# Squared-ReLU attention with routed rows: a table of engines and places for single slots of the middle batches

## The chip, the cores and the metric

One core of a Trainium2 chip runs the whole program. The metric is the device time of one execution in microseconds (us); smaller is better. The engines named below are PE (TensorE matmul, with PEld for its weight loads), ACT (ScalarE), DVE (VectorE), POOL (GpSimd) and SP (SyncE, which issues nearly all transfers).

## The reference, cut to what matters

The inputs are u and v (8 x 3136 x 256), z (8 x 3136 x 64) and the weights of a small network.

```python
scores = (1.0 / S) * np.matmul(z, z.transpose(0, 2, 1))
attn = np.maximum(scores, 0.0) ** 2
x = u * np.matmul(attn, v)
...
for b in range(B):
    top_idx = np.argpartition(-(x[b] @ w_gate), capacity)[:capacity]     # capacity = 128
    xe = x[b, top_idx]
    ye = np.maximum(xe @ w1, 0.0) @ w2
    out[b, top_idx] = xe + sigmoid(xe @ w_gate)[:, None] * ye
```

Nearly all of the arithmetic is in attn times v. The scores matrix is symmetric, so each off-diagonal block of attn is needed twice, once as it is and once transposed.

## The kernel before, in words

**Chunks and slots.** The work goes batch by batch (8 batches). A batch has 7 chunks of output columns: 0 to 4 are 512 wide, 5 is 256 and 6 is 320 wide. A chunk has 13 slots, so a batch has 91, and a slot's number within its batch is its place. Twelve slots of a chunk take two 128-row tiles of v each, the thirteenth takes the last 64 rows. "First batch" is batch 0, "fourth batch" is batch 3.

**One slot.** Products are made in about full precision from a high part and a low part. For a new slot, `scores(k)` has PE make the scores (tile `sc`, one buffer in PSUM), ACT applies ReLU into `a` (line 515) and writes its square, rounded, as the high part `hi` (L525). The exact square is then made in place in `a`, on ACT (L531) or on DVE (L535). `low(k)` makes the low part `lo = a - hi` on POOL or on DVE (both L615) and, where the block is needed again, transposes it on DVE (L578) for a store to `squares`. In the diagonal slot of a chunk (`is_first`) the block is its own mirror, with transposes of its own (L596). For an old slot `old_scores(k)` has the squares fetched back by a transfer into `qk`; ACT makes `hi` from it (L474) and there is no square to make. PE then multiplies into `acc` (L642): 16 matmuls with `hi` and 8 with `lo` in a two-tile slot.

**Order.** The order on every engine is the order in which the program calls the operations; each engine runs its own queue in that order. The main loop goes over the slots. In slot k it runs the plan's loads and preparations, then `mix(k, ...)`, which issues slot k's matmuls and, between them, `scores(k + 3)`. After that come the stores, and the "posts" of the slot with the low parts of slot k + 3 in their middle:

```python
        half = (len(posts) + 1) // 2
        now = settle_scores
        posts = [*posts[:half], now, *posts[half:]]
```

`settle_scores` first makes the squares that were left to DVE, then for each slot its transposes and its low part. In the last two slots of a chunk posts are held over to the next slot.

**Which engine.** A ledger `busy` holds planned microseconds of backlog for ACT, DVE and POOL; `spend` adds to it and each slot takes its own length off. The exact square goes to ACT where ACT's backlog is below DVE's plus 1.0 plus the square's own price. A low part goes to DVE where POOL's backlog would come out 1.2 above DVE's.

**Closing work of a chunk.** In its last two slots `finish_early` scales half of the sums on ACT (L723, two instructions), and `finish` adds the rest on DVE and multiplies by u (L736 and L737, two pairs), which frees the accumulators. What remains goes on the list `near` as two tasks: two transposes to rows on DVE (L746) with a multiply on POOL (L755) and the stores; and a sum on DVE (L764) for the gate. They are taken at slots 2 and 5 of the next chunk (`k % SLOTS % 3 == 2`).

**Routing.** When a batch is finished, `route` and `expert` put its routing and its small network on the list `far`: rounds of a count (DVE, L952 and L958) and a settling, then matmuls. Tasks of `far` are taken in later slots that have no task of `near`, usually every other slot. The first count reads `gates`, which a pair of transfers brings (out at L935, back at L944).

**Preparations.** `prep_v(b, g)` splits a tile of v into its parts, the copy on ACT (L125, 0.6 us) and the rest on POOL (L126); `bring_z(b, c)` does the same for a chunk's moving operand. Both stand in the plan at fixed slots.

Of the kernel before, what the change touches and what calls it, by code (L numbers as in the profile page):

```python
# [22 lines left out]
LEAD = 3  # L23
# [4 lines left out]
BITS = 4  # L28
INT_MIN = -(1 << 31)


# [57 lines left out]
def attention_then_routed_ffn(ctx: ExitStack, tc: tile.TileContext, zt, ut, v, wg, w1, w2, cst, cst16, keys, outs, at, cap):  # L89
# [259 lines left out]
    def prep_v(b, g, on=None, hi_on=None):  # L349

        st = staged["v", b, g // 2][:, g % 2 * 2 :]
        n = 2 if 2 * g < NJ else 1
        if n == 2:
            t = vpool.tile([P, 2, NK, 2 * P], F32R, name="V", tag="V")
        else:
            t = vpool.tile([P, 2, NK, P], F32R, name="Vr", tag="Vr", bufs=1)
        src = st[:, :n].rearrange("p a d -> p (a d)").rearrange("p (f h i) -> p h f i", h=NK, i=Q)
        parts_of = [t[:, w].rearrange("p h (f i) -> p h f i", i=Q) for w in range(2)]
        hi_on = hi_on or on
        lo_on, took = on or nc.gpsimd, {"dve": 1.0} if on else {"pool": 2.3} if hi_on else {"act": 0.6, "pool": 1.3}  # L360
        if not on and b == 0 and n == 2 and busy["pool"] + 1.3 > busy["dve"] + 0.6:
            lo_on, took = nc.vector, {"act": 0.6, "dve": 0.6}
        split(src, *parts_of, hi_on and hi_on.tensor_copy, lo_on.tensor_tensor)
        for q in range(n):
            V[b, 2 * g + q] = t[:, :, :, q * P : (q + 1) * P]
        spend(**took)
# [47 lines left out]
    def is_second(k):  # L414

        b, c, js, _ = slots[k]
        return (b or c) and c < WHOLE and js[0] == c * GT + 2

    parts = {}
    lows = []  # L420
    held_turns = []
    near = deque()
# [55 lines left out]
    def scores(k):  # L478
# [50 lines left out]
        dve = 0.15 + 0.00208 * w  # L529
        if busy["act"] < busy["dve"] + 1.0 + dve + (0.16 + 0.00236 * w if turns(k) else 0.0):  # L530
            nc.scalar.activation(a, a, AF.Square)  # L531
            spend(act=act)
            square = lambda: None
        else:
            square = lambda: nc.vector.tensor_tensor(a, a, a, op=ALU.mult)  # L535
            spend(dve=dve)
# [6 lines left out]
    def low(k, a, hi, pieces, square):  # L543
# [55 lines left out]

        later = 2 * (0.08 + 0.00118 * w) if k >= LEAD and k % (SLOTS * NCH) == 1 else 0.0  # L600
        if k < LEAD or later:
            held_turns.append(lambda: (spend(dve=-later), turned()))
        else:
            turned()
        spend(dve=later)
        if n == 2:
            lo = work.tile([P, 2, CH], F32R, name="lo", tag="lo", bufs=LEAD)[:, :, within(c, k % SLOTS in ((0, 1, 8) if b == B - 1 else (0, 1)))]
            for view, src in pieces:
# [3 lines left out]
                dve = 0.05 + 0.001 * of  # L612
                if busy["pool"] + took > busy["dve"] + dve + (1.2 if busy["pool"] > 0 else 0.0):
                    on, took = nc.vector, dve
                on.tensor_tensor(view(lo), src, view(hi).bitcast(F32), op=ALU.subtract)  # L615
                spend(**{"dve" if on is nc.vector else "pool": took})
        parts[k] = (hi, lo)

# [826 lines left out]
    for b in range(B):  # L1445
        k0 = b * per

        for i in range(NCH):
# [4 lines left out]
            else:  # L1453
                k = k0 - 1 + 4 * (i - WHOLE)
            use = lambda b=b, i=i: prep_z(b, i)
# [8 lines left out]
        for g in range(NJ // 2 + 1):  # L1464
            k = k0 - 10 + 3 * g // 2 if b else max(1, g - 3)
            if b or g > 3:
# [7 lines left out]
        for c in range(NCH):  # L1474
            if b or c:
                at_slot(k0 + c * SLOTS - LEAD - 4, lambda b=b, c=c: bring_z(b, c))
                if c < WHOLE:
# [121 lines left out]
    for k, (b, c, js, is_old) in enumerate(slots):  # L1599
# [8 lines left out]
        if len(js) == 2:  # L1608
            if near and (k % SLOTS or c <= NCH - late if late else k % SLOTS % 3 == 2):
                tasks.append(near.popleft())  # L1610
# [28 lines left out]
        if late and k == len(slots) - 1:  # L1639
            held.reverse()  # L1640
            (f0, s0), (f1, s1) = held
            for op in f0[0][0][:3]:
                op()
        mix(k, [op for ops, _ in tasks for op in ops], lambda: more_scores(k + LEAD))
        settle_turns()
# [94 lines left out]
```

## Time and profile before

| what | us |
|---|---|
| three runs, median (lowest to highest) | 2106.46 (2103.55 to 2107.81) |
| the profiled execution | 2098.54 |
| its span, first to last instruction | 2096.7 |
| PE busy in it | 2024.4 |
| DVE, ACT, POOL busy in it | 1504.4, 1487.4, 1302.3 |

The profile shows one execution, by the chip's clock. An instruction's idle time is how long its engine stood still just before it, and the arrow names what ended the wait. PE's matmuls of one group overlap, so a group's time is that of the group. The middle batches repeat each other nearly to the hundredth of a microsecond, so one batch can stand for the six.

### The profile page before, as it was taken

The page shows a single profiled execution, that of the slowest core. Times are in us where ns is not written, and L with a number is a line of the kernel's source. Part 1 is how long each engine was busy: PE and PEld are TensorE (multiplying, and loading weights), DVE is VectorE, ACT ScalarE, POOL GpSimd, SP SyncE. Part 2 cuts the span into 40 slices and gives each one's busy share as a digit, 9 for nine tenths or more (in the row PEclk, how much of TensorE's full clock was granted, in tenths as well). Part 3 has the DMA queues.
Part 4 walks back from the last instruction along what each step waited for, and adds up shares of the span by engine and source line. Part 5 has one row for each costly group of instructions (what it writes and reads, how often), then busy time and mean ns, then how long its engine had stood idle before and what let it go on. Part 6 is the DMA issues. An engine that isn't in the chain of part 4 may idle for free.

```text
span 2096.7 us, 51099 instructions
## 1 busy us (share of the span) xinstructions
PE 2024.4 (97%) x19700; PEld 1682.5 (80%) x19700; DVE 1504.4 (72%) x2646; ACT 1487.4 (71%) x2028; POOL 1302.3 (62%) x716
## 2 busy tenths in 40 slices
PE   8999999999999999999999999999999999999998
PEld 5788977779787797777977788777887878777787
DVE  9777678756786568865788657885678865866675
ACT  7776688666886578765788657876578766877553
POOL 5765478735786367763678536784467754775643
PEclk9999999999999999999999999999999999999999
DMA  6788767786678966788668886678766777666852
GB/s 178 214 232 223 226 183 226 231 240 192 184 210 225 239 184 185 220 226 224 171 195 222 233 220 190 192 219 229 213 200 198 205 193 212 197 171 178 216 155 93
DMA packets 450868, 426.94 MB, mean 204 GB/s; under 512 B 136576, under 2 KB 377792, under 8 KB 447808
## 3 DMA queue, kind: packets, MB, share of 16 engines
q1 hardware_dynamic: 449488, 421.18, 71.3%
q8 instruction: 154, 2.52, 0.5%
q0 software_dynamic: 768, 2.10, 0.3%
q14 instruction: 90, 0.74, 0.1%
q10 hardware_dynamic: 368, 0.39, 0.1%
HBM read 248.94 MB, written 174.60 MB: 202 GB/s over the span
## 4 chain that ended last, share of the span: by engine, by line
PE 54%; DMA 9%; issue 7%; POOL 7%; ACT 6%; DVE 6%; SPq 5%; POOLq 0%; ACTq 0%; DVEq 0%
PE acc L642 46%; POOL lo L615 5%; PE sc L511 5%; DMA zst<-in_zt 2%; DVE a L535 2%; ACT a L515 2%; ACT hi L525 2%; DMA squares_narrow<-aT 1%; DVE aT L578 1%; SPq L753 1%; DMA qk<-squares 1%; DMA ut<-in_ut 1%; PE y L1402 1%; SPq L446 1%; ACT a L531 1%
## 5 line engine op out<-in xcount | busy, mean ns | idle before, releaser
L642 PE MATMUL acc<-hi,V 64*128 64x512 f32 (+2 forms) x10752 | 1242.5, 362 | 6.8 <-DVE ut L737 4.8
L642 PEld LDWEIGHTS acc<-hi,V 64*128 64x128 f32 x10752 | 952.1, 185 | 171.2 <-issue 13.0
L615 POOL TENSOR_TENSOR lo<-a,hi 128x1024 fp32r<-128x1024 f32 (+1 forms) x280 | 640.2, 2289 | 417.5 <-DVE a L535 173.2
L642 PE MATMUL acc<-lo,V 64*128 64x512 f32 (+2 forms) x5376 | 694.9, 362 | 34.0 <-POOL lo L615 33.6
L642 PEld LDWEIGHTS acc<-lo,V 64*128 64x128 f32 x5376 | 486.1, 185 | 121.2 <-POOL lo L615 52.8
L515 ACT ACTIVATE a<-sc 128x1024 f32<-128x1024 f32 (+2 forms) x345 | 326.8, 947 | 225.8 <-PE sc L511 193.3
L578 DVE STREAM_TRANSPOSE aT<-a 128x512 f32<-128x512 f32 (+1 forms) x494 | 316.2, 680 | 167.7 <-ACT a L531 162.6
L474 ACT CAST hi<-qk 128x1024 fp32r<-128x1024 f32 (+2 forms) x327 | 279.1, 856 | 156.4 <-PE acc L642 112.5
L615 DVE TENSOR_TENSOR lo<-qk,hi 128x1024 fp32r<-128x1024 f32 (+2 forms) x216 | 318.0, 1483 | 68.9 <-ACT hi L474 54.4
L525 ACT ACTIVATE hi<-a 128x1024 fp32r<-128x1024 f32 (+2 forms) x345 | 339.8, 985 | 27.7 <-PE acc L642 5.4
L615 POOL TENSOR_TENSOR lo<-qk,hi 128x1024 fp32r<-128x1024 f32 (+2 forms) x111 | 222.0, 2007 | 128.5 <-ACT hi L474 92.0
L531 ACT ACTIVATE a<-a 128x1024 f32<-128x1024 f32 (+2 forms) x268 | 263.4, 983 | 7.6
L535 DVE TENSOR_TENSOR a<-a 128x1024 f32<-128x1024 f32 (+1 forms) x77 | 135.2, 1756 | 43.6 <-ACT hi L525 38.1
L755 POOL TENSOR_TENSOR ut<-x,w_run 128x1024 f32<-128x1024 f32 (+2 forms) x52 | 130.3, 2506 | 54.6 <-DVE x L746 52.6
L126 POOL TENSOR_TENSOR V<-vst,V 128x512 fp32r<-128x512 f32 x92 | 147.4, 1612 | 23.7 <-ACT V L125 23.7
L736 DVE SCALAR_TENSOR_TENSOR acc<-acc,x 128x512 f32<-128x512 f32 (+2 forms) x112 | 70.0, 625 | 78.7 <-PE acc L642 78.7
L126 POOL TENSOR_TENSOR ZL<-zst,ZH 64x256 fp32r<-64x256 f32 x70 | 69.2, 988 | 70.4 <-ACT ZH L125 52.7
L511 PE MATMUL sc<-Z,ZH 64*128 64x512 f32 x480 | 97.5, 394 | 12.7 <-ACT a L515 12.0
L511 PE MATMUL sc<-Z,ZL 64*128 64x512 f32 x480 | 92.8, 372 | 0.8 <-DVE ZL L126 0.8
L511 PE MATMUL sc<-Zl,ZH 64*128 64x512 f32 x480 | 92.5, 373 | 0.0
L615 DVE TENSOR_TENSOR lo<-a,hi 128x1024 fp32r<-128x1024 f32 (+2 forms) x65 | 75.7, 1165 | 16.7 <-ACT a L531 16.6
L723 ACT ACTIVATE x<-acc 128x512 f32<-128x512 f32 (+2 forms) x112 | 54.4, 538 | 45.3 <-PE acc L642 42.0
(220 smaller groups left out, 1753.0 us busy)
## 6 DMA issues: line engine op xcount, KB each, us to landing
squares<-aT SPq DMA_DIRECT2D x160, 512.0 KB, 3.4
qk<-squares SPq DMA_DIRECT2D x320, 256.0 KB, 6.4
squares_narrow<-aT SPq DMA_DIRECT2D x320, 128.0 KB, 4.3
qk<-squares_narrow SPq DMA_DIRECT2D x80, 512.0 KB, 4.3
out<-x SPq DMA_DIRECT2D x162, 128.0 KB, 3.4
ut<-in_ut SPq DMA_DIRECT2D x40, 512.0 KB, 5.9
vst<-in_v SPq DMA_DIRECT2D x158, 128.0 KB, 3.1
zmv<-in_zt SPq DMA_DIRECT2D x78, 128.0 KB, 4.3
```

The lines of the kernel that those rows point to most:

```text
L126: (lo_on or nc.vector.tensor_tensor)(lo, src, hi.bitcast(F32), op=ALU.subtract)
L474: nc.scalar.copy(by(hi), src)
L511: nc.tensor.matmul(ps[:, q, :w], stationary(high, js[0] // 2, q), mov[m][rows], start=i == 0, stop=i == 2)
L515: nc.scalar.activation(a, ps[:, :, :w], AF.Relu)
L525: nc.scalar.activation(pieces[0][0](hi), pieces[0][1], AF.Square)
L531: nc.scalar.activation(a, a, AF.Square)
L535: square = lambda: nc.vector.tensor_tensor(a, a, a, op=ALU.mult)
L578: nc.vector.transpose(to, a[:, q].rearrange("p (m t a) -> p m t a", m=GT, a=Q))
L615: on.tensor_tensor(view(lo), src, view(hi).bitcast(F32), op=ALU.subtract)
L642: nc.tensor.matmul(bank[g][h][:, cols[g]], V[b, j][rows, i, h], mov[rows], start=(b, c, g, h) not in opened, stop=len(js) == 1 and n == 2,)
L736: nc.vector.scalar_tensor_tensor(rest, rest, SCALE * SCALE, sums[h], op0=ALU.mult, op1=ALU.add)
L755: nc.gpsimd.tensor_tensor(wx, runs, consts["wg_run"].rearrange("p (o r) -> p o r", o=1).broadcast_to([P, NB, RUN]), op=ALU.mult,)
```

## The change

For batches 1 to 6 (the middle ones) a table `PICK` overrides what the ledger or the rule would say in single places: `lo` (True: the low part on DVE, False: on POOL) in eleven, `sq` (True: the exact square on ACT, False: on DVE) in five, `ne` (take a task of `near` or not) in seven, `tl` (True: the transposes are issued behind the low part) in six. Its keys are places, 0 to 90. The ledger still books what is done, so later choices can differ too.

A flag `within_end` is set in the main loop when slot k is one of the last two of its chunk. The scores made there are those of places 1 and 2 of the next chunk; where these are new slots, the exact square goes to ACT, in all batches, unless `PICK` says otherwise.

Two preparations of v move (`VP`: number 8 two slots earlier, number 12 one slot earlier) and `bring_z` of chunk 4 moves two slots later (`BZ`), in all batches but the first. `VD` and `ZP` are all zeros.

```diff
+PICK = {
+    "lo": {
+        1: {1: True, 3: False, 8: True, 11: True, 23: True, 33: True, 44: True, 57: False, 66: False, 69: True, 76: True},
+    },
+    "ne": {
+        1: {4: True, 13: True, 41: False, 42: True, 65: False, 79: True, 83: False},
+    },
+    "sq": {
+        1: {1: False, 3: False, 6: False, 17: True, 48: False},
+    },
+    "tl": {
+        1: {6: True, 8: True, 26: True, 31: True, 46: True, 56: True},
+    },
+}
+VP = [0, 0, 0, 0, 0, 0, 0, 0, -2, 0, 0, 0, -1]
...
+BZ = [0, 0, 0, 0, 2, 0, 0, 0]
...
+    def pick(kind, k, default):
+        b, at = divmod(k, SLOTS * NCH)
+        return PICK.get(kind, {}).get(0 if b == 0 else 2 if b == B - 1 else 1, {}).get(at, default)
...
-        if busy["act"] < busy["dve"] + 1.0 + dve + (0.16 + 0.00236 * w if turns(k) else 0.0):
+        on_act = within_end[0] or busy["act"] < busy["dve"] + 1.0 + dve + (0.16 + 0.00236 * w if turns(k) else 0.0)
+        if pick("sq", k, on_act):
...
+        behind = (turns(k) or is_first(k)) and pick("tl", k, False)
         if k < LEAD or later:
             held_turns.append(lambda: (spend(dve=-later), turned()))
-        else:
+        elif not behind:
             turned()
...
-                if busy["pool"] + took > busy["dve"] + dve + (1.2 if busy["pool"] > 0 else 0.0):
+                if pick("lo", k, busy["pool"] + took > busy["dve"] + dve + (1.2 if busy["pool"] > 0 else 0.0)):
...
+        if behind and not (k < LEAD or later):
+            turned()
...
-            k = k0 - 10 + 3 * g // 2 if b else max(1, g - 3)
+            k = k0 - 10 + 3 * g // 2 + (VP[g] if 0 < b else 0) if b else max(1, g - 3)
...
-                at_slot(k0 + c * SLOTS - LEAD - 4, lambda b=b, c=c: bring_z(b, c))
+                at_slot(k0 + c * SLOTS - LEAD - 4 + (BZ[c] if b else 0), lambda b=b, c=c: bring_z(b, c))
...
-            if near and (k % SLOTS or c <= NCH - late if late else k % SLOTS % 3 == 2):
+            if near and (k % SLOTS or c <= NCH - late if late else pick("ne", k, k % SLOTS % 3 == 2)):
...
+        within_end[0] = k % SLOTS >= SLOTS - 2
         mix(k, [op for ops, _ in tasks for op in ops], lambda: more_scores(k + LEAD))
```

## Rows read from the trace of the kernel before

**Rows 1.** The page, part 1: busy time of each engine.

```profile
PE 2024.4 (97%) x19700; PEld 1682.5 (80%) x19700; DVE 1504.4 (72%) x2646; ACT 1487.4 (71%) x2028; POOL 1302.3 (62%) x716
```

**Rows 2.** Busy time by stretch, the whole fourth batch; length, then each engine.

```profile
781.20:1038.90 257.70, 250.47 (x2455) 208.36 (x2453) 183.17 (x325) 184.81 (x252) 161.71 (x88) 1.00 0.74 209
```

**Rows 3.** Waits of PE over the span: total, times, longest.

```profile
PE acc L642 <- POOL lo L615: 33.6, 37, 2.4
```

**Rows 4.** Groups by line over the span: what a square and a low part take on each engine.

```profile
L615 POOL TENSOR_TENSOR lo<-a,hi 128x1024 fp32r<-128x1024 f32 (+1 forms) x280 | 640.2, 2289 | 417.5 <-DVE a L535 173.2 <-ACT a L531 142.7 <-issue 22.9
...
L531 ACT ACTIVATE a<-a 128x1024 f32<-128x1024 f32 (+2 forms) x268 | 263.4, 983 | 7.6
...
L535 DVE TENSOR_TENSOR a<-a 128x1024 f32<-128x1024 f32 (+1 forms) x77 | 135.2, 1756 | 43.6 <-ACT hi L525 38.1 <-POOL lo L615 5.3
...
L615 DVE TENSOR_TENSOR lo<-a,hi 128x1024 fp32r<-128x1024 f32 (+2 forms) x65 | 75.7, 1165 | 16.7 <-ACT a L531 16.6
```

**Rows 5.** Timeline, fourth batch, chunk 3, diagonal slot: ACT, DVE, POOL, PE.

```profile
907.80 1.06 ACT L525 ACTIVATE hi<-a 128x1024 fp32r<-128x1024 f32 x1
...
911.20 1.22 DVE L535 TENSOR_TENSOR a<-a 128x1024 f32<-128x1024 f32 x1
...
912.49 2.37 POOL L615 TENSOR_TENSOR lo<-a,hi 128x1024 fp32r<-128x1024 f32 x1 [9.70 <-DVE a L535]
...
914.92 1.20 PE L642 MATMUL acc<-lo,V 64*128 64x512 f32 x8 [1.24 <-POOL lo L615]
```

**Rows 6.** Timeline of PE, the same slot of the first and of the last batch.

```profile
151.94 1.20 PE L642 MATMUL acc<-lo,V 64*128 64x512 f32 x8 [1.15 <-POOL lo L615]
...
1939.41 1.19 PE L642 MATMUL acc<-lo,V 64*128 64x512 f32 x8 [1.26 <-POOL lo L615]
```

**Rows 7.** Timeline of PE, chunk 4, diagonal slot: first and last batch.

```profile
191.06 1.19 PE L642 MATMUL acc<-lo,V 64*128 64x512 f32 x8 [0.70 <-POOL lo L615]
...
1984.19 1.19 PE L642 MATMUL acc<-lo,V 64*128 64x512 f32 x8 [2.29 <-POOL lo L615]
```

**Rows 8.** Timeline, fourth batch, chunk 1: DVE, POOL, ACT, then PE.

```profile
833.14 0.62 DVE L952 TENSOR_SCALAR_CACHE_REDUCE ge<-gates,k_sb 128x392 bf16<-128x392 f32 x1 [3.59 <-DMA gates<-scores_there]
...
845.44 0.67 DVE L746 STREAM_TRANSPOSE x<-ut 128x512 f32<-128x512 f32 x1
...
833.89 2.42 POOL L615 TENSOR_TENSOR lo<-a,hi 128x1024 fp32r<-128x1024 f32 x1
...
846.19 2.41 POOL L755 TENSOR_TENSOR ut<-x,w_run 128x1024 f32<-128x1024 f32 x1 [4.25 <-DVE x L746]
...
843.28 1.06 ACT L531 ACTIVATE a<-a 128x1024 f32<-128x1024 f32 x1
...
850.97 1.20 PE L642 MATMUL acc<-lo,V 64*128 64x512 f32 x8 [1.67 <-POOL lo L615]
```

**Rows 9.** Timeline, fourth batch, start of chunk 0: ACT, DVE, then PE.

```profile
781.44 1.06 ACT L531 ACTIVATE a<-a 128x1024 f32<-128x1024 f32 x1
...
785.74 1.02 ACT L515 ACTIVATE a<-sc 128x1024 f32<-128x1024 f32 x1
...
785.36 3.13 DVE L535 TENSOR_TENSOR a<-a 128x1024 f32<-128x1024 f32 x1 [2.70 <-ACT hi L525]
...
784.29 0.51 PE L511 MATMUL sc<-Z,ZH 64*128 64x512 f32 x2 [0.94 <-ACT a L515]
...
788.32 0.39 PE L511 MATMUL sc<-Z,ZH 64*128 64x512 f32 x2
...
792.18 0.50 PE L511 MATMUL sc<-Z,ZH 64*128 64x512 f32 x2 [0.30 <-ACT a L515]
```

**Rows 10.** Timeline, fourth batch, place 9 of chunk 0: POOL, DVE, then PE.

```profile
814.98 4.64 POOL L615 TENSOR_TENSOR lo<-a,hi 128x1024 fp32r<-128x1024 f32 x2
...
815.58 2.87 DVE L615 TENSOR_TENSOR lo<-zst,hi 128x512 fp32r<-128x512 f32 x1
...
817.96 1.19 PE L642 MATMUL acc<-lo,V 64*128 64x512 f32 x8 [0.72 <-POOL lo L615]
```

More of the change, by code (lines that the diff above doesn't have):

```diff
@@ L29 @@
 INT_MIN = -(1 << 31)
+PICK = {
[13 more added lines that the diff above has]
+VP = [0, 0, 0, 0, 0, 0, 0, 0, -2, 0, 0, 0, -1]
+VD = [0, 0, 0, 0, 0, 0, 0, 0, 0, 0, 0, 0, 0]
+ZP = [0, 0, 0, 0, 0, 0, 0, 0]
+BZ = [0, 0, 0, 0, 2, 0, 0, 0]
 def chunks_of(S):
@@ L362, in prep_v @@
             lo_on, took = nc.vector, {"act": 0.6, "dve": 0.6}
+        if b and VD[g]:
+            lo_on, took = nc.vector, {"act": 0.6, "dve": 0.6}
         split(src, *parts_of, hi_on and hi_on.tensor_copy, lo_on.tensor_tensor)
@@ L417, in is_second @@
         return (b or c) and c < WHOLE and js[0] == c * GT + 2
+    def pick(kind, k, default):
+        b, at = divmod(k, SLOTS * NCH)
+        return PICK.get(kind, {}).get(0 if b == 0 else 2 if b == B - 1 else 1, {}).get(at, default)
     parts = {}
     lows = []
+    within_end = [False]
     held_turns = []
@@ L1453, in attention_then_routed_ffn @@
             else:
-                k = k0 - 1 + 4 * (i - WHOLE)
+                k = k0 - 1 + 4 * (i - WHOLE) + ZP[i]
             use = lambda b=b, i=i: prep_z(b, i)
```

## Prediction

> **What bounds the kernel now.** I read the page first: PE is busy 2024.4 us of the span of 2096.7 [rows 1], so what can be won without taking work from PE is the 72.3 us in which it stands still, and the change takes no matmul away. Then the stretches by batch: the fourth batch lasts 257.70 us with PE busy 250.47 [rows 2], so a middle batch loses some 7 us, while DVE, ACT and POOL are busy 162 to 185 us of it. No other engine is near its limit over a batch; PE waits at single places where one of them is late. The view of PE's waits says for whom: 33.6 us in 37 waits for low parts on POOL, the largest item by far [rows 3]. Then I followed the timeline of the fourth batch to each such wait, and looked for the same place in the other batches. Nearly all of them sit at five places, and they recur.
>
> *Diagonal slots of chunks 3 and 4 (places 40 and 53).* In chunk 3 PE waits 1.24 us for a low part that ran from 912.49 to 914.86 on POOL, which had idled 9.70 us before it. The cause is one step back: ACT had written the high part by 908.86, but the exact square is on DVE, whose queue holds the closing work of the chunk before (L736 and L737, two pairs). The square starts only at 911.20 [rows 5]. The wait stands in all eight batches, 1.15 in the first and 1.26 in the last [rows 6], the six between at 1.24 to 1.25: 9.9 us. In chunk 4 it has the same form: 0.70 to 0.72 in the first six batches, 0.12 in the seventh, 2.29 in the last [rows 7]: 6.7 us. Together 16.6 us.
>
> *Place 19 of chunk 1.* PE waits 1.67 us for a low part that stood on POOL behind the multiply L755 (2.41 us); this had waited for the second closing transpose on DVE, 845.44 to 846.11, while POOL idled 4.25 us. DVE in turn had idled 3.59 us, until 833.14, with the first count of the routing at the head of its queue waiting for its transfer [rows 8]. The wait is there in five of the six middle batches, 1.64 to 1.68: 8.3 us.
>
> *Places 0 and 2.* PE waits 0.94 us for a ReLU on ACT, which ahead of it made an exact square (781.44, 1.06 us), and at place 2 0.30 us (0.34 in the other batches) for the next but one [rows 9]; there ACT waited for a buffer whose reader on DVE stood behind a square that took 3.13 us. That is 1.28 us in a middle batch: 7.7 in six.
>
> *Place 9.* 0.72 us for a low part on POOL [rows 10], 0.16 to 0.72 in the middle batches, 2.7 us together.
>
> **The change part by part.** (a) *Squares of places 1 and 2 on ACT.* At places 40 and 53 the square leaves the queue of closing work. At place 40 ACT starts it at 908.89, ahead of the old slot's high part, which moves back by its 1.06, and ends at about 909.95; POOL is idle, so the low part ends 2.37 later, at 912.3, and PE came for it at 914.92 - 1.24 = 913.68. It is 1.4 us early: the wait goes, and the delayed high part of slot 41 still has PE's 24 matmuls of slot 40 ahead of it. At place 53 the same steps hold. Removed: 16.6 us. The flag has no table behind it, so this holds in all batches. DVE is spared 1.22 us each time.
>
> (b) *Closing tasks of chunk 0 at places 13 and 15 in place of 15 and 18, those of the chunk before at 2 and 4.* The two transposes of place 13 enter DVE's queue before the routing's later rounds, so L755 comes to POOL about three low parts earlier. Counting 2.41 us an instruction from the end of the low part of slot 16 (836.30), the multiply and the low parts of 17 and 18 are done by 843.5; the low part of 19 then starts when its square is made (on ACT, 844.34) and ends at 846.8; PE wants it at 850.97 - 1.67 = 849.30 [rows 8]. Slack 2.5 us: the wait of 8.3 us goes in five batches. The routing also starts one slot earlier, its count being held over to slot 12 as before by the rule for the last two slots, and its later rounds gain up to three slots; its transfers are issued a slot earlier, so DVE's 3.59 us should shrink. I take 7.0 of the 8.3, because L755 now sits in front of three low parts.
>
> (c) *Chunk 0: squares 1 and 3 and low parts 1, 8 and 11 to DVE, low part 3 to POOL, square 2 to ACT.* ACT comes to the ReLU that PE waited for 0.94 us that much earlier. But the square of slot 2 (0.98 mean [rows 4]) and the copy of v number 8 (0.6) now come before the next ReLU, which ended at 786.76 for matmuls at 788.32 [rows 9]: it ends 0.98 + 0.6 - 0.94 = 0.64 later, at 787.4, while PE comes for it 0.94 or somewhat more earlier, at 787.4 or before. PE waits 0 to 0.6 there, at place 1; I take 0.6. The square that took 3.13 on DVE is gone there, and so is the 0.34 at place 2. Net 0.94 + 0.34 - 0.6 = 0.7 us a batch, 4 in six. Bounds: 0, if DVE's two new jobs come late, to 7.7. The load of v number 8 stands only one slot ahead of its copy now; if it lands late ACT waits for it, inside these bounds.
>
> (d) *Place 9.* POOL loses low parts 1 and 8 and gains 3: one of 2.29 us less [rows 4], against 0.72 missing. But PE comes up to 2 us earlier after (c). I take 1.5 of 2.7; bounds 0 and 2.7.
>
> (e) *The rest.* Transposes behind a low part matter only where both are on DVE (6, 8, 26); three entries of the other kind change nothing, since POOL's queue is another one. Low parts 23, 33, 44, 69 and 76 leave POOL for DVE (2.29 against 1.17 us alone [rows 4]) and 57 goes back; square 48 goes to DVE. None is at a place where PE waits in the fourth batch, and DVE has a quarter of the batch idle to take them [rows 2]. Moving `bring_z` of chunk 4 leaves three slots before its use. I price (e) and all that moves with the ledger at 2 us of new waits in the whole run (bounds 0 and 10: one wait of 1.6, like that at place 19, in each middle batch).
>
> One rule speaks against (c) and (e). On DVE a low part takes 1.17 us in the mean [rows 4], but one of half the elements took 2.87 with POOL at work beside it [rows 10]; a square takes 3.13 there [rows 9] and 1.22 alone [rows 5]. The Trainium skill (SBUF — State Buffer, section "SBUF: two separate sides") says that VectorE instructions with two SBUF inputs and GpSimd hold one pair of ports by turns, for a whole instruction, the other fully blocked. The trace agrees. By it alone, work moved off POOL would help only by its shorter length, and the sum would be that of the first rival.
>
> **The sum.** 16.6 + 7 + 4 + 1.5 - 2 = 27 us. The profiled execution took 2098.5 us, 1.8 of it around the span, and would take 2071.5. It was 8 us faster than the median of the three runs shown, 2106.46; taking the same 27 us from that gives 2079.5.
>
> **The rivals.** *DVE and POOL in each other's way.* The jobs moved in chunk 0 collide: (c) and (d) come to nothing, and new waits cost 4 instead of 2. For it: the 2.87 and 3.13 above. Against: DVE idled 2.70 us before the 3.13 [rows 9], and that square is the one that leaves. 16.6 + 7 - 4 = 20 us, 2086.5; chance 0.22.
>
> *The waits only move.* PE, no longer held, meets the next late low part, and all but a few microseconds come back. For it: low parts follow each other on POOL without a gap. Against: at places 40 and 53 POOL had idled and is ahead by 1.4 us afterwards. 2104, chance 0.12.
>
> *Slower: the routing's count blocks DVE at the end of chunk 0.* It is issued with its settling in one slot, ahead of the transposes of slots 15 and 16 and of the closing transposes. If its transfer lands no earlier than now, DVE waits the 3.59 us again [rows 8] with more queued behind, buffers of `a` come free late, and ReLU and PE stand. It decides against the change once that costs over 4.5 us in each middle batch (27 / 6); at 5.5 the time is 2112. Against: DVE's wait cost PE almost nothing there before. Chance 0.08.
>
> **Numbers.** The forecast has 0.58, and its own range is 2070 to 2090. With the rivals, 2066 (all 35.3 us of the five places, 5 of the 37 us of PE's idle time elsewhere, nothing new) to 2103. A difference of 0.2%, some 4 us, is about what a measurement of this kernel can tell from none. Faster by more: 0.58 + 0.22 = 0.80; within it 0.12; slower 0.08.
>
> **What would show it.** (a) The exact squares of places 40 and 53 on ACT at L531's new line and no wait of PE for POOL there, in all eight batches; DVE's squares fewer. (b) L755 of chunk 0 before the low part of slot 18, and no wait at place 19. (c) The wait of 0.94 gone, and one of about 0.6 at place 1 in its stead. (d) Place 9 below 0.5. PE's waits for low parts on POOL should fall from 33.6 to some 10, with PE's busy time as before. The forecast is wrong if PE waits for low parts on DVE by more than 5 us in all, or if the middle batches still lose 5 us or more each.

## The result, and the profile after

| | before | after |
|---|---|---|
| median of four runs (us) | 2105.01 | 2048.38 |
| lowest to highest | 2099.85 to 2107.81 | 2046.65 to 2055.07 |
| ratio, 95% interval | | 0.974 [0.9709, 0.977] |
| span of the profiled execution | 2096.7 | 2044.8 |
| PE busy in it | 2024.4 | 2008.1 |

The change wins 51.9 us of span, about twice the 27 forecast; the medians lie 56.6 us apart. It is faster, as predicted, but below the range (2066 to 2103). Run once more beside one of the experiments, the same kernel took 2047.97 (ratio 0.9741 [0.9727, 0.9756]). The nine executions of the changed kernel have spans of 2044.6 to 2053.3 us, so a few microseconds between two single executions say little. Medians and ratios leave out one slow execution of the flag alone, of 10555.56 us.

The helper lines have moved: ReLU L515 is now L540, the high part L525 is L550, the square L531 on ACT is L557 and L535 on DVE is L561, the low part L615 is L642, the matmuls into `acc` L642 are L671; L746, L755 and L952 are L775, L784 and L981.

The page, part 1, of the changed kernel, against [rows 1]:

```profile
PE 2008.1 (98%) x19700; PEld 1717.6 (84%) x19700; DVE 1507.5 (74%) x2660; ACT 1496.8 (73%) x2032; POOL 1271.7 (62%) x698
```

The number of matmuls is the same, 19700, yet PE's *busy* time has fallen by 16.3 us; its idle time fell from 72.3 to 36.7, by 35.6. The prediction had said "PE's busy time as before". Here is half of the surprise.

A little of the 16.3 is PE's granted clock. Around the start, in the first and in the last batch it stood at 0.5 (1.2 GHz) for three stretches before and two after, the last 3.6 us of the run left out. Here is one of each, before and after: length, then PE, PEld, DVE, ACT, POOL, granted clock.

```profile
54.13:60.96 6.83, 6.27 (x30) 4.43 (x28) 6.79 (x6) 1.50 (x3) 6.83 (x4) 0.50 0.40 104
53.36:56.77 3.41, 3.21 (x16) 2.09 (x14) 3.38 (x4) 0.97 (x3) 3.41 (x2) 0.50 0.47 142
```

PE is busy 12.52 us in the three and 6.62 in the two; half of the difference, some 3 us, is my estimate of the clock's share. In the repeat of the changed kernel such stretches hold 12.92 us of PE's work, as much as before, and PE is busy 2010.0: still 14.4 less.

PE's waits after, against [rows 3] (total, times, longest):

```profile
PE acc L671 <- POOL lo L642: 7.4, 12, 2.4
PE sc L536 <- ACT a L540: 6.6, 10, 1.1
PE acc L671 <- DVE ut L766: 4.4, 10, 0.5
```

Waits for low parts on POOL went from 33.6 us in 37 to 7.4 in 12. Neither sign that was to speak against the forecast appeared: waits for low parts on DVE stay at 0.3 us, and the middle batches lose 0.9 to 2.9 us each. These batches are less alike than was said at the start: before, they last 248.8 to 259.9 us, and PE idles 5.0 to 9.5 us in them. The fourth batch, against [rows 2]: length, then PE, PEld, DVE, ACT, POOL.

```profile
762.48:1012.73 250.25, 248.61 (x2454) 209.30 (x2452) 185.25 (x328) 185.95 (x252) 156.38 (x85) 1.00 0.76 215
```

It is 7.45 shorter, and PE's idle time in it went from 7.23 to 1.64.

Place 40 of the fourth batch, against [rows 5]; timeline of ACT, DVE, POOL, PE:

```profile
885.89 1.06 ACT L557 ACTIVATE a<-a 128x1024 f32<-128x1024 f32 x1
886.85 1.03 ACT L499 CAST hi<-qk 128x1024 fp32r<-128x1024 f32 x1
...
885.52 0.70 DVE L765 SCALAR_TENSOR_TENSOR acc<-acc,x 128x512 f32<-128x512 f32 x1 [2.40 <-PE acc L671]
...
887.03 2.41 POOL L642 TENSOR_TENSOR lo<-a,hi 128x1024 fp32r<-128x1024 f32 x1 [7.23 <-ACT a L557]
...
888.70 1.98 PE L671 MATMUL acc<-hi,V 64*128 64x512 f32 x16
890.51 1.07 PE L671 MATMUL acc<-lo,V 64*128 64x512 f32 x8
```

The square stands on ACT ahead of the old slot's high part, while DVE does the closing work; the low part ends at 889.44, PE comes for it at 890.51. The slack is 1.07 (forecast 1.4) and the wait is gone, in all eight batches, as is that of place 53 [rows 6, 7].

Place 19, against [rows 8]; DVE, POOL, PE:

```profile
811.63 0.62 DVE L981 TENSOR_SCALAR_CACHE_REDUCE ge<-gates,k_sb 128x392 bf16<-128x392 f32 x1 [3.46 <-DMA squares_narrow<-aT]
...
816.17 0.67 DVE L775 STREAM_TRANSPOSE x<-ut 128x512 f32<-128x512 f32 x1
...
816.93 2.40 POOL L784 TENSOR_TENSOR ut<-x,w_run 128x1024 f32<-128x1024 f32 x1 [1.99 <-ACT hi L550]
819.29 9.49 POOL L642 TENSOR_TENSOR lo<-a,hi 128x1024 fp32r<-128x1024 f32 x4
...
821.76 1.20 PE L671 MATMUL acc<-lo,V 64*128 64x512 f32 x8 [0.33 <-POOL lo L642]
```

The multiply L784 now comes ahead of four low parts, those of slots 17 to 20. The third of them ends at some 826.4 (three quarters of 9.49), and PE comes for it at 828.01: 1.6 us of slack and no wait at place 19. Slot 17, first behind the multiply, is the one that pays: 0.33 here, 1.24 in the six batches together. DVE still waits 3.46 us at the first count. The trace puts that down to a store, squares_narrow; in [rows 8] it names `gates`, which the instruction reads, and I take it to be that here too.

The start of chunk 0, against [rows 9]; ACT, DVE, PE:

```profile
763.43 1.02 ACT L540 ACTIVATE a<-sc 128x1024 f32<-128x1024 f32 x1
...
763.88 2.30 DVE L561 TENSOR_TENSOR a<-a 128x1024 f32<-128x1024 f32 x1
...
763.91 0.73 PE L671 MATMUL acc<-lo,V 64*128 64x512 f32 x4 [0.35 <-POOL lo L642]
764.50 0.50 PE L536 MATMUL sc<-Z,ZH 64*128 64x512 f32 x2
```

The wait of 0.94 for the ReLU is gone: it ends at 764.45, just before the matmuls of 764.50. What stays is a wait of 0.35 for a low part of POOL ahead of it; it was there before, 0.38 at 782.62, and is counted in none of my terms. At place 9, against [rows 10], POOL ends the low part at 794.98 and PE reads it at 796.68, without a wait.

```profile
792.03 2.95 POOL L642 TENSOR_TENSOR lo<-a,hi 128x1024 fp32r<-128x1024 f32 x1
...
796.68 1.09 PE L671 MATMUL acc<-lo,V 64*128 64x512 f32 x8
```

### The profile page after: what moved, and what is told of

It reads as the page before. It is cut to its first block, busy times and chain, and to the rows that moved or that the text cites. A ratio compares the mean times of both kernels' runs of the same rounds, so it can differ in the third digit from the quotient of the medians.

```text
span 2044.8 us, 51027 instructions
## 1 busy us (share of the span) xinstructions
PE 2008.1 (98%) x19700; PEld 1717.6 (84%) x19700; DVE 1507.5 (74%) x2660; ACT 1496.8 (73%) x2032; POOL 1271.7 (62%) x698
## 4 chain that ended last, share of the span: by engine, by line
PE 85%; DVE 5%; ACT 3%; DMA 3%; issue 2%; SPq 1%; POOL 1%; POOLq 0%; DVEq 0%; ACTq 0%
PE acc L671 72%; PE sc L536 9%; DVE a L561 1%; DMA vst<-in_v 1%; PE h L1388 1%; ACT a L540 1%; ACT hi L550 1%; PE y L1431 1%; POOL lo L642 1%; PE sc L519 1%; DVE aT L604 1%; DMA qk<-squares_narrow 1%; DVE lo L642 1%; DVE ut L766 0%; DVE acc L765 0%
## 5 line engine op out<-in xcount | busy, mean ns | idle before, releaser
L671 PE MATMUL acc<-hi,V 64*128 64x512 f32 (+2 forms) x10752 | 1249.1, 362 | 6.4 <-DVE ut L766 4.4
L671 PEld LDWEIGHTS acc<-hi,V 64*128 64x128 f32 x10752 | 976.1, 185 | 150.2 <-issue 12.9
L642 POOL TENSOR_TENSOR lo<-a,hi 128x1024 fp32r<-128x1024 f32 (+2 forms) x249 | 573.6, 2307 | 408.1 <-ACT a L557 259.8
L671 PE MATMUL acc<-lo,V 64*128 64x512 f32 (+2 forms) x5376 | 697.5, 360 | 7.7 <-POOL lo L642 7.4
L671 PEld LDWEIGHTS acc<-lo,V 64*128 64x128 f32 x5376 | 503.9, 184 | 72.9 <-POOL lo L642 12.7
L540 ACT ACTIVATE a<-sc 128x1024 f32<-128x1024 f32 (+2 forms) x345 | 327.1, 948 | 199.3 <-PE sc L536 188.2
L550 ACT ACTIVATE hi<-a 128x1024 fp32r<-128x1024 f32 (+2 forms) x345 | 339.9, 985 | 23.9 <-PE acc L671 5.1
L642 DVE TENSOR_TENSOR lo<-qk,hi 128x1024 fp32r<-128x1024 f32 (+2 forms) x210 | 307.7, 1476 | 64.2 <-ACT hi L499 47.2
L642 POOL TENSOR_TENSOR lo<-qk,hi 128x1024 fp32r<-128x1024 f32 (+2 forms) x117 | 229.6, 1969 | 139.3 <-ACT hi L499 83.1
L557 ACT ACTIVATE a<-a 128x1024 f32<-128x1024 f32 (+2 forms) x272 | 273.3, 1005 | 8.0
L144 POOL TENSOR_TENSOR V<-vst,V 128x512 fp32r<-128x512 f32 x92 | 159.0, 1739 | 30.1 <-ACT V L143 29.3
L642 DVE TENSOR_TENSOR lo<-a,hi 128x1024 fp32r<-128x1024 f32 (+1 forms) x96 | 139.6, 1454 | 31.5 <-ACT a L557 26.5
L784 POOL TENSOR_TENSOR ut<-x,w_run 128x1024 f32<-128x1024 f32 (+2 forms) x52 | 118.5, 2279 | 49.4 <-DVE x L775 44.7
L561 DVE TENSOR_TENSOR a<-a 128x1024 f32<-128x1024 f32 (+1 forms) x73 | 110.4, 1513 | 25.2 <-ACT hi L550 20.8
L144 POOL TENSOR_TENSOR ZL<-zst,ZH 64x256 fp32r<-64x256 f32 x70 | 77.0, 1101 | 48.6 <-ACT ZH L143 34.3
```

What stands on the lines that cost most here:

```text
L144: (lo_on or nc.vector.tensor_tensor)(lo, src, hi.bitcast(F32), op=ALU.subtract)
L540: nc.scalar.activation(a, ps[:, :, :w], AF.Relu)
L550: nc.scalar.activation(pieces[0][0](hi), pieces[0][1], AF.Square)
L671: nc.tensor.matmul(bank[g][h][:, cols[g]], V[b, j][rows, i, h], mov[rows], start=(b, c, g, h) not in opened, stop=len(js) == 1 and n == 2,)
L784: nc.gpsimd.tensor_tensor(wx, runs, consts["wg_run"].rearrange("p (o r) -> p o r", o=1).broadcast_to([P, NB, RUN]), op=ALU.mult,)
```

## Where the time came from

I measured each slot from its first matmul with `hi` to that of the next slot, in both traces, and beside it the idle time of PE in the slot.

| step, places | forecast | idle time less | slots shorter by |
|---|---|---|---|
| (a) 40, 53, 54 in eight batches | 16.6 | 17.2 | 22.95 |
| (b) 16 to 20, middle batches | 7.0 | 7.45 | 9.76 |
| (c) 0 to 3, middle batches | 4.0 | 7.08 | 9.05 |
| (d) 7 to 10, middle batches | 1.5 | 2.74 | 5.03 |
| (e) and all else (the rest of the span) | -2.0 | | 5.1 |
| sum | 27.1 | | 51.9 |

The last row is no measure of (e) alone: it also holds the rest of the first and last batch with their clock, and 2.0 us of it is one wait at place 35 of batch 1.

Slot length fell by more than idle time, and at the cleanest places by the same amount for each wait that went. Place 40: idle 1.24, slot 4.25 to 2.72, so 1.53. Place 53: 0.72 and 1.00 to 1.03. Place 19: 1.67 and 1.96. Place 2: 0.34 and 0.62. Each time some 0.29 more than the profile calls idle. Place 3 shows it without any idle time: none before and none after, yet its six slots are 1.32 shorter. At place 9 the surplus is larger, 0.39 to 0.42: there two small matmuls of the routing went from the end of slot 8 to the end of slot 7, with the closing tasks. The group behind such a pair also starts slowly, 2.11 for 16 matmuls instead of 1.98. That move is also why slot 7 grew by 0.38. My theory before the experiments: **a wait costs its idle time and some 0.28 us.** The trace of before shows where this sits. Timeline of PE, then of PEld, at place 40:

```profile
911.70 1.98 PE L642 MATMUL acc<-hi,V 64*128 64x512 f32 x16
...
914.92 0.76 PEld L642 LDWEIGHTS acc<-lo,V 64*128 64x128 f32 x8 [1.66 <-POOL lo L615]
```

Pairs of these matmuls start every 0.223 us, but a matmul lasts 0.386. So 16 matmuls hold PE for 1.98 and the next group starts, when nothing is late, 1.81 after the first: in the changed kernel 888.70 and 890.51. The last pair is still counted as busy for some 0.16 us in which the next pair should have begun; idle time starts only after that. And after a wait, the weight load has stopped too (1.66 idle against PE's 1.24), and the second pair starts 0.33 after the first in place of 0.22: the group of eight takes 1.20 in [rows 5] and 1.07 above. 0.16 + 0.11 = 0.27, and a wait under 0.16 us shows no idle time at all.

## The experiments

Spans are of one profiled execution; ratios are to runs of the kernel before on the same chip. "Growth" of a slot is against the kernel named.

### The flag alone, the closing tasks alone, chunk 0 alone

Three runs put one part each into the kernel before.

```diff
+        on_act = within_end[0] or busy["act"] < ...        # e1_flag: PICK empty, VP and BZ zero
```
```diff
+PICK = {'ne': {1: {4: True, 13: True, 41: False, 42: True, 65: False, 79: True, 83: False}}}     # e2_closing
```
```diff
+PICK = {'lo': {1: {1: True, 3: False, 8: True, 11: True}},                                       # e3_chunk0
+        'sq': {1: {1: False, 2: True, 3: False, 6: False}}, 'tl': {1: {6: True, 8: True}}}
+VP = [0, 0, 0, 0, 0, 0, 0, 0, -2, 0, 0, 0, -1]
```

> The kernel before with the flag alone (exact squares of places 1 and 2 of a chunk on ACT; no table, nothing moved in the plan). Theory: a wait of PE costs its idle time in the view plus about 0.28 us, because the last pair of matmuls still counts as busy for 0.16 us (each lasts 0.39 but is issued every 0.22) and the first pair after it comes 0.11 late. All sixteen waits at places 40 and 53 go: PE idle falls by 16.6 us and the span by some 21 (40: 1.53 a batch, 53: 1.0). Rival: the idle time is the whole price, and what PE's busy time lost in the full change came from the other parts: the span falls by 16.6, PE's busy time stays within 1 us.

> The kernel before with the seven entries for closing tasks alone. Theory (idle plus 0.28 for each wait): place 19 shortens by 1.96 in five batches, the span falls by some 10 us with idle falling 8.3. Rival (idle alone): 8.3. If the entry for place 13 works only together with the table's other entries (squares and low parts of chunk 0), the wait at place 19 stays and the span falls by less than 4.

> The kernel before with the entries for chunk 0 alone: squares 1, 3 and 6 on DVE and 2 on ACT, low parts 1, 8 and 11 on DVE and 3 on POOL, transposes 6 and 8 behind the low part, the two preparations of v moved. Theory: the waits at places 0, 2 and 9 go with what they cost beside their idle time: idle falls by some 10 us, the span by 14. Rival (idle alone): 10. Rival of the prediction (DVE and POOL in each other's way in chunk 0): less than 5.

| | median us | ratio [95%] | span less by | the slots it is for |
|---|---|---|---|---|
| flag | 2076.86 | 0.9886 [0.9851, 0.9921] | 21.6 | 40: -9.20; 53, 54: -6.0; 2, 3: -5.1; 8, 9: +5.0 |
| closing tasks | 2088.86 | 0.9937 [0.9919, 0.9954] | 8.0 | 19: -10.05 |
| chunk 0 | 2090.79 | 0.9949 [0.993, 0.9969] | 10.5 | 0: -6.39; 2, 3: -4.8; 9: -4.36; 1: +3.05 |

(Slots of the six middle batches.) Place 40 is the cleanest: 7.47 us of idle time went and 9.20 of slot length, with the flag alone as with everything. The span of the flag alone fell by 21.6, PE's busy time by 10.6, against 16.6 and at most 1 if idle time were the whole price. The other two spans fell short of the 10 and 14 expected and don't decide: each part also lost in places it isn't for, the closing tasks 3.5 in the last batch, which their table does not touch. Over the six middle batches they gave 11.0 and 12.6. The three spans sum to 40.1, the whole change gives 51.9, though the flag's and chunk 0's gains at places 2 and 3 are counted twice in the sum. So the parts cover each other: the flag alone loses 5.0 at places 8 and 9 again. Timeline of POOL and PE with the flag alone, fourth batch:

```profile
804.33 2.38 POOL L629 TENSOR_TENSOR lo<-a,hi 128x1024 fp32r<-128x1024 f32 x1
...
808.36 4.65 POOL L629 TENSOR_TENSOR lo<-a,hi 128x1024 fp32r<-128x1024 f32 x2
...
806.76 1.20 PE L658 MATMUL acc<-lo,V 64*128 64x512 f32 x8 [0.56 <-POOL lo L629]
...
811.36 1.19 PE L658 MATMUL acc<-lo,V 64*128 64x512 f32 x8 [0.72 <-POOL lo L629]
```

PE, ahead by the flag's gain, meets POOL's low parts of chunk 0, which are no earlier: the rival "the waits only move", at this place and at this size. The entries for chunk 0, low parts 1 and 8 on DVE among them, remove it at place 9 and half of it at place 8, as the next run shows; which entry does it was not isolated.

### Flag and chunk 0 together

```diff
+PICK = {'lo': {1: {1: True, 3: False, 8: True, 11: True}},      # and the flag, and VP; no 'ne'
+        'sq': {1: {1: False, 3: False, 6: False}}, 'tl': {1: {6: True, 8: True}}}
```

> The flag and the entries for chunk 0 together, closing tasks at their old slots. With the flag alone PE came earlier to places 8 and 9 of chunk 0 and waited there for low parts on POOL (5.0 us given back in six batches); alone, the chunk-0 entries take low parts off POOL there. Theory (the parts cover each other): places 7 to 9 fall by 4 us or more against before, the wait at place 19 stays, and the span is 2096.7 - 21.6 - 10.5 + 5.1 (square 2 is in both) - 7 (what the flag gave back or more) = some 2063. Rival (the parts simply add, square 2 once): 2070.

2063.88, ratio 0.9826 [0.9801, 0.9852], span 2060.7. Places 7 to 9 are 2.7 shorter than before where the flag alone had given back 5.0; 4 or more were expected, and place 8 still loses 1.7. The wait at place 19 stays (8.34). The span fits the theory that the two parts complete each other (2063), not the plain sum (2070).

### A wait of a known size

Part of low part 40 of the changed kernel is made twice on POOL, in each middle batch a larger part, so that its end passes PE's need by a different amount.

```diff
+LATER = {91 + 40: 208, 182 + 40: 232, 273 + 40: 256, 364 + 40: 320, 455 + 40: 416, 546 + 40: 512}
+                if k in LATER and on is nc.gpsimd:
+                    n = LATER[k]
+                    on.tensor_tensor(lo[:, :, :n], a[:, :, :n], hi[:, :, :n].bitcast(F32), op=ALU.subtract)
                 on.tensor_tensor(view(lo), src, view(hi).bitcast(F32), op=ALU.subtract)
```

> The kernel after, with a part of the low part of place 40 made twice on POOL in the middle batches (416, 464, 512, 640, 832 and 1024 elements of it in batches 1 to 6), which makes it later by some 1.0 to 2.4 us against a slack of 1.07. Theory: once PE is late by d, slot 40 grows by about d plus 0.12, of which the view shows only d less 0.16 as idle; so growth less idle is 0.28 at every dose past 0.16, and a small dose lengthens the slot with no idle shown. Rival: growth equals the idle shown. In either case no slot before 40 changes.

| batch | 1 | 2 | 3 | 4 | 5 | 6 |
|---|---|---|---|---|---|---|
| slot 40 longer by | 0.27 | 0.376 | 0.484 | 0.744 | 1.15 | 1.588 |
| idle shown | 0 | 0.092 | 0.196 | 0.455 | 0.866 | 1.284 |
| difference | 0.27 | 0.284 | 0.288 | 0.289 | 0.284 | 0.304 |

Timeline of PE in batches 1 and 6 of this run:

```profile
391.95 1.19 PE L675 MATMUL acc<-lo,V 64*128 64x512 f32 x8
...
1647.65 1.21 PE L675 MATMUL acc<-lo,V 64*128 64x512 f32 x8 [1.28 <-POOL lo L646]
```

At this place that settles the theory against the one that PE's busy time is unchanged by a wait: over a range of 0 to 1.28 of idle time the surplus is 0.27 to 0.30. The first row is the instructive one: no idle time is printed, yet the group takes 1.19 in place of 1.07, and the slot is 0.27 longer. Such a wait is in no list of waits.

### The later entries

```diff
-        1: {1: True, 3: False, 8: True, 11: True, 23: True, 33: True, 44: True, 57: False, 66: False, 69: True, 76: True},
+        1: {1: True, 3: False, 8: True, 11: True},       # likewise 'ne', 'sq', 'tl': only places below 14
-BZ = [0, 0, 0, 0, 2, 0, 0, 0]
+BZ = [0] * 8
```

> The kernel after without the rest: no table entries from place 14 on (low parts 23, 33, 44, 57, 66, 69, 76, squares 17 and 48, transposes 26, 31, 46, 56, closing tasks from place 41 on) and the moving operand of chunk 4 at its old slot. Theory: the rest is worth little where PE did not wait; span within 4 us of the 2044.8 after. Rival: the rest carries a good part of the 12 us that the three parts tried alone (21.6, 8.0 and 10.5 us of the span) leave of the 51.9: span above 2051.

2054.53, ratio 0.9784 [0.9763, 0.9805]; span 6.3 above the changed kernel's where 4 at most was expected, 5.0 of it in batch 1. At place 35 there PE waits 2.05 for a scan of the routing on DVE, as it did before the change; in the changed kernel it does not. So (e), priced as a loss of 2, is a gain of a few microseconds, near the limit of what the runs can tell (the interval overlaps the changed kernel's first, [0.9709, 0.977], and just misses its second, [0.9727, 0.9756]) and in one batch only.

### The copy of v number 8 back in its slot

```diff
-VP = [0, 0, 0, 0, 0, 0, 0, 0, -2, 0, 0, 0, -1]
+VP = [0, 0, 0, 0, 0, 0, 0, 0, 0, 0, 0, 0, -1]
```

> The kernel after with the preparation of v number 8 back at its old slot. The prediction charged its 0.6 us on ACT to the ReLU of place 1, which the kernel after has late (0.29 to 1.0 us of slot length). If that is so, place 1 falls to 3.40 in all middle batches, 3 us together, and something is lost at places 2 to 9 where ACT and POOL make the copy instead. Rival: the ReLU is late for another reason and place 1 stays.

2059.88, ratio 0.9809 [0.9785, 0.9832], span 12.6 above the changed kernel's. Place 1 became 2.58 shorter in six, as step (c) has it: the copy is what holds that ReLU. But place 7 grew by 6.88, with 5.29 of waits for low parts, now on DVE, and batch 1 by 7.5 in all, some 1.5 of it at a lower granted clock at place 25 (last section). The move of this preparation is worth more than it costs.

### More low parts to DVE, booked, then unbooked

The obvious next step is the wait of 0.35 at place 0, the largest that still recurs at places 0 to 20 of the middle batches, and the one at place 17.

```diff
+    'lo': {1: {..., 0: True, 17: True}, 2: {0: True, 1: True}}, 'sq': {..., 2: {1: False}},          # e7_more
+    'tl': {1: {..., 0: True}, 2: {0: True}}
```
```diff
+MOVED = {91 * b + at for b in range(1, 7) for at in (0, 15)} | {637, 638}                            # e9_unbooked
...
+                booked = {"dve" if on is nc.vector else "pool": took}
+                if k in MOVED:
+                    on = nc.vector
...
+                spend(**booked)
```

> The kernel after with four more entries in the middle batches (low parts 0 and 17 on DVE, transposes 0 behind the low part) and, in the last batch, low parts 0 and 1 on DVE, square 1 on DVE and transposes 0 behind the low part. By the price of idle plus 0.28: place 0 gives 0.34 + 0.28 in six batches (3.7), place 17 gives 2.1 in the three batches where it waits, the last batch 1.5: 7 us off 2044.8, so 2038. By idle alone: 2.0 + 1.2 + 1.2 = 4.4. Rival: DVE is late itself by the two low parts and ReLU waits for buffers; no gain.

> The changed kernel with low parts 0 and 15 of the middle batches and 0 and 1 of the last on DVE instead of POOL, transposes 0 behind the low part, and the square of place 1 of the last batch on DVE; the ledger books all of it as before, so no later choice differs. Theory (a wait costs its idle time and some 0.28 us more, and entries fail only when the ledger sends other squares elsewhere): the wait at place 0 of the middle batches (2.02 us in six, so 2.02 + 6 x 0.28 = 3.7) goes, up to 2 us of place 17 and 1.5 of the last batch; the span falls by 4 to 7 us against the changed kernel. Rival (DVE and POOL in each other's way: two more DVE instructions beside POOL just where DVE has the closing work only move the waits to places 1 and 2 and 17): the span is within 2 us of the changed kernel's or longer.

> The changed kernel once more, unchanged, on the same chip as the run with the unbooked low parts, for a direct comparison. Every theory expects its time of before, 2048 us, a ratio of 0.974 and the same waits place by place.

Both failed. The booked one: 2056.53, ratio 0.9789 [0.9763, 0.9815], span 11.4 above the changed kernel's. I laid this to the ledger, which sent other squares elsewhere (66 on DVE in place of 73). The unbooked one left no such choice open, and came out worse: 2065.0, ratio 0.9828 [0.9811, 0.9846], beside 0.9741 for the unchanged table on the same chip. It is not quite the same set, since it moves low part 15 instead of 17; but its loss at place 1 is the same, so for that the reason fell. In both, place 0 kept its length with a wait for ReLU in place of that for POOL, and place 1 grew by 6 us in the six middle batches; ahead of that ReLU, ACT waited 1.39 us (booked) and 1.64 us (unbooked) for a transfer of v in the fourth batch. In the unbooked run slot 15 grew by 7.4 in six as well, with 5.6 of waits for its low part on DVE. Two last runs took low part 0 alone, with its transposes in front and behind.

```diff
+MOVED = {91 * b for b in range(1, 7)}                            # e11_lo0; e12_lo0_tl0 adds 'tl' {1: {0: True}}
```

> The changed kernel with low part 0 of the six middle batches on DVE, unbooked, and nothing else; its transposes stay ahead of it. Theory (the loss of the run with four unbooked low parts came from SP's queue: the transposes behind the low part made the store of squares some 1.04 us late, the loads of v behind it on SP late, and ACT waited 1.64 us for one of them ahead of a ReLU): with the transposes in front the loads go as before, the wait of place 0 (2.02 us in six slots, 3.7 with 0.28 each) goes, place 1 stays within 1 us in six, and the span falls by 3 to 4 us against the changed kernel. Rival (the low part itself is too much for DVE beside the closing work and POOL): place 1 grows by 4 us or more here too.

> As the run with low part 0 alone on DVE, but with the transposes of place 0 behind it. Theory: the store of squares issues some 1 us later on SP, the loads of v behind it too, ACT idles over 1 us ahead of the copy of v and place 1 grows by some 6 us in the six middle batches; the span is 2 to 8 us above the changed kernel's. Rival: no different from the run with the transposes in front.

Transposes behind: 2057.69, ratio 0.9788 [0.9765, 0.9812], place 1 longer by 8.4 in six where some 6 were expected, and the span 12.1 above the changed kernel's instead of 2 to 8. Two of the six batches lost 1.6 each at a lower granted clock behind the wait (last section). Timeline of DVE, SP, ACT and PE, fourth batch:

```profile
769.71 0.77 DVE L613 STREAM_TRANSPOSE aT<-a 128x256 f32<-128x256 f32 x2
...
770.51 0.36 SPq L615 DMA_DIRECT2D squares_own<-aT  x1
770.96 1.83 SPq L349 DMA_DIRECT2D vst<-in_v  x4
...
776.01 0.62 ACT L131 CAST V<-vst 128x512 fp32r<-128x512 f32 x1 [1.71 <-DMA vst<-in_v]
...
777.61 0.50 PE L524 MATMUL sc<-Z,ZH 64*128 64x512 f32 x2 [1.79 <-ACT a L528]
```

Transposes in front: 2052.64, ratio 0.976 [0.9738, 0.9782], place 1 within 0.3 of the changed kernel's:

```profile
770.05 0.77 DVE L613 STREAM_TRANSPOSE aT<-a 128x256 f32<-128x256 f32 x2
...
770.85 0.36 SPq L615 DMA_DIRECT2D squares_own<-aT  x1
771.30 1.83 SPq L349 DMA_DIRECT2D vst<-in_v  x4
...
773.20 0.50 PE L524 MATMUL sc<-Z,ZH 64*128 64x512 f32 x2 [0.49 <-ACT a L528]
```

Slot 0 begins at 769.62 in the first and at 771.17 in the second. Measured from there, the store of the squares leaves at +0.89 and at -0.32: 1.21 us later, the length of the low part that was put in front of its transposes. The loads of v stand behind that store in SP's queue, ACT's copy waits 1.71 for one, the ReLU stands behind the copy, and PE behind the ReLU. That part of the theory is shown: four instructions that are on nobody's list of costs, tied by two queues.

The other part fell. With the transposes in front, place 0 still did not become shorter (4.20 as before): the low part's wait gave way to one of 0.49 for the ReLU of the next scores. The changed kernel's rows say so beforehand: its ReLU at 763.43 ends at 764.45, the matmuls that need its buffer begin at 764.50. The wait for the low part covers a second one that is nearly as long. Places 8 and 23 to 25 of batch 1 cost 7 more, so the whole gains nothing. No version here beats the changed kernel.

The loss in batch 1 looks like the slower rival, in one batch. Timeline of DVE, POOL and PE, batch 1, with low part 0 on DVE:

```profile
313.18 0.62 DVE L975 TENSOR_SCALAR_CACHE_REDUCE ge<-gates,k_sb 128x392 bf16<-128x392 f32 x1 [3.04 <-DMA squares_narrow<-aT]
...
339.90 2.70 DVE L636 TENSOR_TENSOR lo<-a,hi 128x512 fp32r<-128x512 f32 x1
342.52 1.75 DVE L636 TENSOR_TENSOR lo<-vst,hi 128x512 fp32r<-128x512 f32 x1
...
339.65 2.40 POOL L636 TENSOR_TENSOR lo<-a,hi 128x1024 fp32r<-128x1024 f32 x1 [1.38 <-issue]
342.00 1.72 POOL L132 TENSOR_TENSOR wl<-vst,wh 128x512 fp32r<-128x512 f32 x1
...
344.33 1.20 PE L665 MATMUL acc<-lo,V 64*128 64x512 f32 x8 [1.62 <-DVE lo L636]
```

and the same instructions on DVE in the changed kernel:

```profile
311.14 0.62 DVE L981 TENSOR_SCALAR_CACHE_REDUCE ge<-gates,k_sb 128x392 bf16<-128x392 f32 x1 [1.29 <-DMA squares_narrow<-aT]
...
338.01 0.69 DVE L642 TENSOR_TENSOR lo<-a,hi 128x512 fp32r<-128x512 f32 x1
338.62 0.69 DVE L642 TENSOR_TENSOR lo<-vst,hi 128x512 fp32r<-128x512 f32 x1
```

DVE waits 1.75 us longer for `gates`, comes 1.89 us later to the two halves of low part 23, and there meets POOL's work: each half lasts until POOL's instruction beside it is done (342.05 and 343.72), and 0.55 more, 4.4 us for the two instead of 1.3. This is what the Trainium skill (SBUF — State Buffer, section "SBUF: two separate sides") says of VectorE instructions with two SBUF inputs and GpSimd, that one blocks the other for a whole instruction; the rows agree. Why `gates` comes later in that run I did not trace. In the five runs that lost in batch 1 (5.0 to 8.3 us) the first count started 49.5 to 50.4 us after the batch's start; in the two of the changed kernel 47.1 and 47.2. That the one causes the other was not isolated, and lateness alone doesn't do it: in the changed kernel's batch 4 the first count starts 50.0 us after the batch's start, without such a loss. In two of the five runs some 1.5 us of the loss is a lower granted clock at place 25 (last section).

## Why the prediction was right and wrong

**What bounds the kernel:** right. Of the 35.3 us listed at the five places, the slots around them gave back 34.5 as idle time, net of the new waits there; all of PE lost 35.6.

**The step that failed:** a wait was priced at the idle time that the profile prints, with "PE's busy time as before". A wait costs 0.27 to 0.30 us more, shown by the run with graded delays at place 40 and fitting at places 2, 19 and 53, and that is half of the 24.8 us that the forecast missed. In the table above this is the difference of the last two columns over (a) to (d), 46.8 - 34.5 = 12.3 us. The other half is size: 5.4 more idle time at the four steps than forecast, mostly in (c), and 7.1 in the last row. The Trainium skill (Perfetto Trace Analysis, section "Identifying the Most-Contended Engine") warns that the busy share of matmuls is a poor measure of how close TensorE is to its limit, because matmuls are pipelined, and says in "Tensor Engine Instruction (MATMUL, LD_WEIGHTS)" that their end times are modelled. The runs agree: the same 19700 matmuls were busy 16.3 us less, some 3 of it the clock's. It gives no price for a wait; that is from the runs here. Because it went by idle time, even the outer bound, 2066, was too high: it was worked out as all 35.3 us of the five places and 5 more, and no case in the range went past the idle time.

**(a)** Right in mechanism and in every slot; 16.6 forecast, 17.2 of idle time, 22.95 with the surplus. The flag alone brings it. It also cures place 2, whose square on ACT the prediction listed under (c).

**(b)** Right: wait gone, slack 1.6 where 2.5 was forecast, the multiply L784 ahead of the low part of slot 17, and the 1.3 kept back for that nearly all spent at slot 17 (idle time +1.08, slots +1.13). DVE's wait for `gates` shrank, but hardly in the fourth batch (3.59, now 3.46); over the six it went from 24.0 to 16.6.

**(c)** Mis-sized: 4 forecast, 9.05 measured, 7.08 of it idle time. The new wait at place 1 is there for the reason given, since it falls when the copy of v goes back; it is 0.13 us of idle time in the mean (0.81 in six) in place of 0.6, and by slot length 0.43 (2.57 in six). The upper bound that I gave, 7.7, was nearer. The 0.94 at place 0 went.

**(d)** Mis-sized: all 2.74 of idle time went, 1.5 was taken, and the slots gave 5.03. The closing tasks have a share in it: alone they shorten place 9 by 1.44. The 1.17 us that the prediction called a low part alone on DVE is a mean over two shapes, 1.28 for a whole one and 0.94 for half; the sum doesn't hang on it.

**(e)** Wrong in sign, by a few microseconds.

**The rivals.** *DVE and POOL in each other's way*: not in the sum, though seen in single rows (2.30 for a square, 2.70 for half a low part). *The waits only move*: wrong for the whole, right for the parts: the flag alone gives back 5.0, each attempt to move further low parts gave back all and more. *The routing's count blocks DVE*: DVE does wait for `gates`, 1.29 to 3.71 us in the changed kernel's middle batches, at no visible cost; in batch 1 a count 2.4 to 3.4 us later went together with losses of 5 to 8. The forecast of no such cost held for the change as made.

## What to carry to other kernels

Price a wait by the length of the slot with and without it, not by the idle time in the list; where short matmuls overlap, add the overlap and the restart, and look for groups that take longer than their like (1.19 against 1.07) though no idle time is printed. A wait may hide a second one behind it: before removing it, look up what PE needs next and when that is ready. And when a step moves on one engine, follow what it issues: a transpose 1.2 us later made a store late, the store a load, the load a copy, the copy a ReLU.

## What the hardware showed beyond that

PE's surplus for a wait at place 40 is constant, 0.27 to 0.30 us, whatever the wait's length between 0 and 1.3 us, and the first group after it takes 1.19 to 1.21 for eight matmuls in place of 1.07. In the profile 0.16 of it is in the matmuls before the wait, which overlap nothing, and some 0.12 in those behind it.

A longer wait can cost more. In the middle batches of the runs here the granted clock fell to 0.5 (1.2 GHz) eight times, each time 0.6 to 1.6 us after the end of a wait of PE of 1.77 to 2.20 us; not every such wait was followed by it. The run with transposes behind, after the wait of 1.79 at 777.61 shown above:

```profile
778.73:782.14 3.41, 3.41 (x20) 2.66 (x18) 3.38 (x4) 3.07 (x3) 2.18 (x2) 0.50 0.59 202
779.84 3.08 PE L665 MATMUL acc<-hi,V 64*128 64x512 f32 x16
```

The group takes 3.08 instead of 1.98. In that run places 1 and 2 grew by their idle time in four batches, and by 1.6 more in the two in which the clock fell.
